# Gated linear attention with a gated projection behind it: scores and state sums of a chunk in 64-token halves, two batches at a time, in a new order of the work

## The chip, the cores and the metric

One of the eight cores of a Trainium2 chip runs the kernel. The metric is the device time of one execution in microseconds (us), taken as the median of several. The engines are PE (TensorE: matrix products, with PEld for the loading of their weights), DVE (VectorE), ACT (ScalarE), POOL (GpSimd) and SP (SyncE, which here only issues DMAs). Each works through its own instructions in order and waits on semaphores for the others.

## The reference

```python
B, H, S, D = q.shape                      # 4, 8, 768, 48
f = 1.0 / (1.0 + np.exp(-f_logit))
for t in range(S):                        # state: [B, H, D, D]
    state = f[:, :, t, :, None] * state + np.einsum('bhd,bhe->bhde', k[:, :, t], v[:, :, t])
    y[:, :, t] = np.einsum('bhd,bhde->bhe', q[:, :, t], state)
x = y.transpose(0, 2, 1, 3).reshape(B, S, H * D)          # 384 channels
gate = 1.0 / (1.0 + np.exp(-causal_conv(x, conv_w)))      # 5 taps, each channel alone
out = ((gate * (x @ w_val)) @ w_out).astype(np.float32)
```

The recurrence runs over 768 tokens for each of 32 (batch, head); the projection with its convolution takes its result. Everything is float32.

## The kernel before

**Chunks.** The 768 tokens are cut into 6 chunks of 128 (`C`). Heads go in pairs, one head on partitions 0 to 47 and the other on 64 to 111, so that there are 16 (batch, pair), `BP`, four pairs in each of four batches. q, k and f lie in HBM as 112 rows of 16 x 128 numbers to a chunk, v as 128 rows (tokens) of 16 x 112. In a chunk, ACT makes -log f (`pexp`, `pln`), DVE sums it along the tokens (`scan`), ACT makes the products of f (`exp1`, in `E1`) and one over them (`exp2`, in `E2`), and DVE multiplies q and k with them (`pmulq`, `pmulk`). These work on halves of 8 (batch, pair), three smaller spans in the first chunk.

**Batches.** What follows goes batch by batch, 24 times in all (chunk c, batch b):

- `scores`: eight products of 48 rows, k times q, 128 tokens against 128 tokens, into the two banks `aps`; `mask`: DVE multiplies all 128 x 1024 of them with the triangle `tri` into `ASB`.
- `ktrans`: four transposes of k into the bank `kps`; `kevac`: ACT copies them out to `KSB`. `dstate`: k times v summed over the 128 tokens into the bank `dps`, two batches side by side.
- For two batches together, `stadd` (DVE) adds `dps` to the state `ss`, `stmul` (POOL) multiplies with the chunk's decay, and `stcopy` (ACT) copies the two heads as blocks of a diagonal into `st`.
- `apply`: y from the state (`st` times q) and from the chunk's own tokens (v times `ASB`), in four lanes of 32 output rows, into one of two banks `xps`; `xevac`: ACT copies y into `XF`.

**The projection.** For each chunk, in three blocks of 128 channels: the convolution (`mlast` on ACT, then four `mconv` on DVE into `gt`), its sigmoid (`gate`), the value product `mval` (nine products of 128 x 128 by 128 x 512: x and w_val are each split in a high and a low part, `xH`, `xL`, `wvH`, `wvL`, by `msplit` and `mlow`), `mmul` on DVE, the split of the result (`mhigh` on ACT, `mrest` on DVE), the output product `mout` (nine products) and `mstore` (ACT, then a DMA). The last chunk's projection is done in two halves of two batches, which the program numbers 5 and 6, in 256 columns. The weights come as float64 bits and are turned into two float32 parts by POOL, ACT and DVE (`weight`). All these products write to two banks `mps`, in the last chunk also to the banks that the others have left.

**Order.** The list `PROGRAM` names the pieces one by one. PE, DVE and ACT do their pieces in exactly this order (class `Ordered`; hence nearly all instructions of the profile carry that helper's line, L113, and are told apart by their tiles' names). SP and POOL get their instructions from the framework's scheduler. All loads and stores go through SP, with at most eight DMAs under way: each waits for the eighth before it to land.

At the end a count tells whether every decay stayed in range; if not, a slow general path computes all anew. It isn't taken here.

Of the kernel before, what the change touches and what calls it, by code (L numbers as in the profile page):

```python
# [21 lines left out]
C = 128  # L22
NC = S // C
BP = B * NP
KT = 5
HALO = KT - 1
NM = DM // 128
#: a chunk's decay products have to stay above this for q * e and k / e to be formed apart
RANGE = 2.0**-58
# [3 lines left out]
WHOLE = [(0, BP)]  # L33
# [3 lines left out]
PROGRAM = """  # L37
halo 0; loadf 0 0; loadf 0 1; busy 10; loadq 0 1; loadq 0 0; loadk 0 0; loadv 0 0; pexp 0 0; loadk 0 1; loadq 0 2;
pln 0 0; loadf 1 0; scan 0 0; loadv 0 1; pexp 0 1; busy 4; loadk 0 2; exp2 0 0; pln 0 1; wload 0; exp1 0 0; busy 4;
loadk 1 0; pmulk 0 0; pexp 0 2; loadq 1 0; pmulq 0 0; ktrans 0 0; loadv 0 2; scan 0 1; pln 0 2; scores 0 0; exp2 0 1;  # L40
scan 0 2; wload 1; exp1 0 1; busy 4; kevac 0 0; pmulq 0 1; exp2 0 2; dstate 0 0; pmulk 0 1; busy 4; exp1 0 2;
mask 0 0; loadv 1 0; ktrans 0 1; loadf 2 0; okc 0; kevac 0 1; pmulq 0 2; scores 0 1; pexp 1 0; weight 0; pmulk 0 2;
apply 0 0; pln 1 0; mask 0 1; loadf 3 0; loadk 2 0; dstate 0 1; wload 2; ktrans 0 2; scores 0 2; kevac 0 2; scan 1 0;
xevac 0 0; stadd 0 0; exp2 1 0; ktrans 0 3; mask 0 2; apply 0 1; kevac 0 3; pmulk 1 0; scores 0 3; stcopy 0 0;
scan 1 1; xevac 0 1; exp1 1 0; ktrans 1 0; loadk 2 1; mask 0 3; apply 0 2; exp2 1 1; loadq 2 0; pmulq 1 0; exp1 1 1;
apply 0 3; loadv 2 0; weight 1; weight 0; xevac 0 2; weight 0; pmulq 1 1; scores 1 0; xevac 0 3; weight 1; halo 1;
msplit 0; weight 1; loadq 2 1; weight 1; dstate 0 2; mask 1 0; dstate 0 3; kevac 1 0; ktrans 1 1; weight 0; stadd 0 1;
scores 1 1; kevac 1 1; pmulk 1 1; loadv 2 1; pexp 2 0; weight 0; weight 1; dstate 1 1; weight 1; apply 1 0; okc 1;
mask 1 1; weight 1; loadf 4 0; pln 2 0; weight 1; mlow 0; weight 3; ktrans 1 2; loadk 3 0; scores 1 2; xevac 1 0;
stcopy 0 1; scan 2 0; apply 1 1; mask 1 2; exp2 2 0; exp1 2 0; weight 0; scan 2 1; weight 2; scores 1 3; loadq 3 0;  # L50
mlast 0 0; pmulk 2 0; xevac 1 1; weight 2; exp2 2 1; mconv 0 0 0; dstate 1 0; mask 1 3; apply 1 2; loadv 3 0;
kevac 1 2; exp1 2 1; pmulq 2 0; ktrans 1 3; pmulq 2 1; scores 2 0; loadk 3 1; kevac 1 3; xevac 1 2; mconv 0 0 1;
weight 3; mlast 0 1; stadd 1 0; ktrans 2 0; weight 2; mlast 0 2; dstate 1 2; stmul 1 0; weight 3; dstate 1 3;
# [12 lines left out]
exp1 4 0; weight 6; mask 3 2; mhigh 0 1; mhigh 0 0; mrest 0 1; dstate 3 1; loadq 5 0; weight 6; mrest 0 0; scores 3 3;
mhigh 0 2; loadv 5 0; weight 6; mlast 1 0; mrest 0 2; mlast 1 1; pmulk 4 0; mout 0 1; msplit 1; mconv 1 0 0;
mconv 1 0 1; mlast 1 2; mout 0 0; mconv 1 1 0; mstore 0 1; mconv 1 0 2; mconv 1 1 1; mout 0 2; mstore 0 0; mlow 1;
ktrans 3 2; mconv 1 0 3; mval 1 0; kevac 3 2; mconv 1 1 2; mstore 0 2; mconv 1 2 0; gate 1 0; stadd 3 0; ktrans 3 3;
mconv 1 1 3; stmul 3 0; mval 1 2; loadk 5 1; mconv 1 2 1; gate 1 1; mmul 1 0; stcopy 3 0; mconv 1 2 2; mval 1 1;  # L70
mhigh 1 0; mconv 1 2 3; kevac 3 3; stcopy 2 1; scan 4 1; halo 3; xevac 3 0; dstate 3 3; xevac 3 1; pmulq 4 0;
dstate 3 2; gate 1 2; apply 3 2; exp2 4 1; stadd 3 1; okc 3; mask 3 3; stmul 3 1; ktrans 4 0; mmul 1 2; pexp 5 0;
scores 4 0; mrest 1 0; mmul 1 1; pmulk 4 1; apply 3 3; mhigh 1 1; mhigh 1 2; mask 4 0; kevac 4 0; exp1 4 1;
dstate 4 0; mrest 1 1; loadq 5 1; mlast 2 0; scores 4 1; loadv 5 1; mrest 1 2; stcopy 3 1; mconv 2 0 0; pln 5 0;
mconv 2 0 1; mout 1 1; mask 4 1; msplit 2; scan 5 1; ktrans 4 1; mout 1 2; xevac 3 2; pmulq 4 1; exp2 5 1; mlow 2;
exp1 5 1; scores 4 2; kevac 4 1; mstore 1 1; pmulq 5 1; mlast 2 2; ktrans 4 2; mout 1 0; kevac 4 2; mconv 2 2 0;
mlast 2 1; mconv 2 0 2; xevac 3 3; scan 5 0; apply 4 0; mconv 2 0 3; exp2 5 0; mconv 2 1 0; exp1 5 0; dstate 4 1;
mconv 2 1 1; apply 4 1; gate 2 0; mask 4 2; pmulk 5 1; mstore 1 0; scores 4 3; mconv 2 2 1; mconv 2 2 2; mval 2 0;
mask 4 3; mstore 1 2; mconv 2 1 2; mval 2 1; mconv 2 2 3; mmul 2 0; pmulq 5 0; mhigh 2 0; ktrans 4 3; mval 2 2;
pmulk 5 0; kevac 4 3; gate 2 2; okc 4; stadd 4 0; scores 5 0; stmul 4 0; msplit 3; mmul 2 2; mconv 2 1 3; mrest 2 0;  # L80
mhigh 2 2; halo 4; dstate 4 2; xevac 4 0; dstate 4 3; mrest 2 2; stcopy 4 0; apply 4 2; stadd 4 1; xevac 4 1;
stmul 4 1; gate 2 1; mlast 3 2; mmul 2 1; apply 4 3; xevac 4 2; mask 5 0; mlast 3 0; mconv 3 0 0; apply 5 0;
mconv 3 0 1; xevac 4 3; mhigh 2 1; mconv 3 0 2; stcopy 4 1; mlow 3; scores 5 1; okc 5; mrest 2 1; mval 3 1; mlast 3 1;
mask 5 1; mconv 3 0 3; mval 3 0; mconv 3 2 0; gate 3 0; mconv 3 2 1; mconv 3 2 2; scores 5 2; mmul 3 0; mconv 3 2 3;
mval 3 2; mask 5 2; mconv 3 1 0; scores 5 3; msplit 4; mconv 3 1 1; mconv 3 1 2; gate 3 2; apply 5 1; mconv 3 1 3;
mmul 3 2; gate 3 1; halo 5; mmul 3 1; mout 2 0; xevac 5 1; mask 5 3; xevac 5 0; mlast 5 2; mlow 4; msplit 5; mout 2 2;
mlast 5 1; mstore 2 0; mlast 5 0; mconv 5 1 0; mlow 5; mout 2 1; mconv 5 0 0; mconv 5 0 1; mconv 5 2 0; mconv 5 0 2;
apply 5 3; mconv 5 1 1; mhigh 3 1; mconv 5 2 1; mhigh 3 2; mhigh 3 0; mrest 3 2; mconv 5 0 3; apply 5 2; mlast 4 2;
mrest 3 1; mstore 2 1; mconv 5 2 2; xevac 5 3; mrest 3 0; mconv 5 1 2; mlast 4 0; mval 4 0; mconv 5 1 3; mconv 4 0 0;
gate 5 1; xevac 5 2; mconv 4 0 1; mstore 2 2; mval 5 0; mlast 6 1; mconv 4 0 2; mlast 6 2; msplit 6; mout 3 0;  # L90
mconv 6 2 0; mconv 4 0 3; mlast 6 0; mlast 4 1; mconv 6 0 0; gate 4 0; mconv 6 0 1; mval 5 2; mconv 4 1 0; mstore 3 0;
# [33 lines left out]
def gla_moe(ctx: ExitStack, tc: tile.TileContext, q, k, f, v, wv, cw, wo, out):  # L125
# [292 lines left out]
    def general(ctx):  # L418
# [21 lines left out]
        for t in (qf, kf, ff):  # L440
            DVE.memset(t, 0.0)
# [203 lines left out]
```

## Time and profile before

| | us |
|---|---|
| time, median of 3 (lowest, highest) | 220.92 (220.72, 226.4) |
| span of the profiled execution | 227.6 |
| PE busy | 184.2 |
| DVE busy | 191.7 |
| ACT busy | 144.0 |
| POOL busy | 32.4 |

For the profiled execution the page gives its span, from the first to the last instruction, and no other time; that span lies 3.0% above the median of the timed runs and 0.5% above the highest. "Busy" counts the time in which at least one instruction of the engine was under way. PE's products overlap one another in their pipeline, so that its busy time is more than the sum of the steps from one product to the next. A float32 product shows as two records of PE, a transpose as one.

### The profile page before, as it was taken

The numbers are of one execution on the slowest core, as the hardware profiler recorded it, in microseconds if no ns is written. First come the engines' busy times: TensorE is split into PE (matmuls) and PEld (weight loads), VectorE is DVE, ScalarE is ACT, GpSimd is POOL, SyncE is SP. The second block draws the span as 40 slices with busy tenths as digits, with TensorE's granted clock in tenths as the row PEclk, the third lists the DMA queues.
The fourth block names the chain that finished last, engine by engine and source line by source line (L and its number), as shares of the span: only waits on it lengthen the run. The fifth ranks groups of instructions, "written<-read, shape, count | busy, mean of one in ns | idle before, by whom it ended". The sixth has DMA issues, their size and how long they took to land.

```text
span 227.6 us, 5654 instructions
## 1 busy us (share of the span) xinstructions
PE 184.2 (81%) x2437; PEld 148.5 (65%) x2438; DVE 191.7 (84%) x251; ACT 144.0 (63%) x226; POOL 32.4 (14%) x37
## 2 busy tenths in 40 slices
PE   7298689649198847775999987979879999999990
PEld 3156568438087736665787875767867788889880
DVE  5395989497499999999997999997799999998800
ACT  4677764686249298967639998553941858553630
POOL 4001011200044842240115100001200000000000
PEclk9959959976979999998599999979999999999998
DMA  6999999999959902244023050120000012111241
GB/s 190 280 254 268 333 336 278 238 239 258 240 129 278 250 15 84 81 164 143 21 92 128 3 164 0 49 95 0 4 3 0 1 49 79 62 50 42 103 152 37
DMA packets 9183, 29.54 MB, mean 130 GB/s; under 512 B 1200, under 2 KB 2224, under 8 KB 8112
## 3 DMA queue, kind: packets, MB, share of 16 engines
q1 hardware_dynamic: 9152, 29.12, 44.5%
q8 instruction: 21, 0.34, 0.6%
q14 instruction: 10, 0.08, 0.1%
HBM read 24.39 MB, written 4.72 MB: 128 GB/s over the span
## 4 chain that ended last, share of the span: by engine, by line
DVE 33%; PE 27%; DMA 24%; ACT 9%; issue 3%; SPq 2%; DVEq 0%; ACTq 0%
PE mps L113 19%; DMA qb<-in_q 10%; DVE gt L113 10%; DMA vb<-in_v 9%; DVE e L113 6%; DMA fb<-in_f 5%; DVE asb L113 5%; ACT e L113 3%; PE aps L113 3%; DVE qb L113 2%; DVE cb L113 2%; PE xps L113 2%; DVE ca L113 2%; DVE kb L113 2%; SPq L178 2%
## 5 line engine op out<-in xcount | busy, mean ns | idle before, releaser
L113 ACT ACTIVATE e<-e 112x1024 f32<-112x1024 f32 (+3 forms) x40 | 39.9, 1003 | 15.0 <-DVE e L113 14.6
L113 DVE SCALAR_TENSOR_TENSOR gt<-xf,cws,gt 128x512 f32<-128x512 f32 x60 | 45.2, 772 | 0.6
L113 PE MATMUL aps<-qb,kb 48*128 48x128 f32 x384 | 31.5, 310 | 13.3 <-DVE asb L113 11.9
L113 PE MATMUL xps<-asb,vb 128*32 128x128 f32 x768 | 38.2, 293 | 1.1 <-DMA vb<-in_v 0.7
L113 PEld LDWEIGHTS aps<-qb,kb 48*128 48x128 f32 x384 | 26.6, 210 | 19.0 <-DVE asb L113 14.2
L113 PE MATMUL xps<-qb,st 112*32 112x128 f32 x480 | 31.7, 287 | 4.7 <-issue 2.9
L113 PEld LDWEIGHTS xps<-asb,vb 128*32 128x32 f32 x768 | 32.8, 119 | 2.6 <-DMA vb<-in_v 1.0
L113 DVE TENSOR_TENSOR_SCAN e<-keep,e 112x1024 f32<-112x1024 bf16 (+1 forms) x13 | 28.7, 2218 | 5.2 <-ACT e L113 5.0
L113 PE MATMUL mps<-rg,woH 128*128 128x512 f32 (+1 forms) x102 | 32.3, 401 | 0.3 <-DVE gt L113 0.3
L113 DVE TENSOR_TENSOR asb<-aps,tri 128x1024 f32<-128x1024 f32 x24 | 29.1, 1213 | 0.0
L113 PEld LDWEIGHTS xps<-qb,st 112*32 112x32 f32 x480 | 22.2, 114 | 7.4 <-issue 3.9
L113 PEld LDWEIGHTS mps<-rg,woH 128*128 128x128 f32 x102 | 19.1, 199 | 4.6 <-DVE gt L113 0.5
L113 PE MATMUL mps<-xH,wvH 128*128 128x512 f32 x45 | 19.2, 428 | 3.1 <-DVE gt L113 2.9
L113 PE MATMUL mps<-rg,woL 128*128 128x512 f32 (+1 forms) x51 | 20.1, 395 | 0.0
L113 DVE TENSOR_TENSOR kb<-kb,e 112x1024 f32<-112x1024 f32 (+1 forms) x13 | 15.4, 1184 | 5.2 <-DMA kb<-in_k 5.2
L113 PE MATMUL mps<-xL,wvH 128*128 128x512 f32 x45 | 18.5, 410 | 0.9 <-DVE xL L113 0.9
L351 POOL TENSOR_TENSOR ss<-u,e 112x384 f32<-112x384 f32 x8 | 9.4, 1173 | 67.2 <-DVE u L113 63.3
L113 DVE TENSOR_TENSOR qb<-qb,e 112x1024 f32<-112x1024 f32 (+1 forms) x13 | 14.7, 1130 | 4.6 <-DMA qb<-in_q 4.6
L113 PE MATMUL mps<-xH,wvL 128*128 128x512 f32 x45 | 18.5, 411 | 0.0
L113 PE MATMUL dps<-vb,ksb 128*48 128x48 f32 x320 | 11.7, 226 | 7.6 <-DVE u L113 5.1
L113 PEld LDWEIGHTS dps<-vb,ksb 128*48 128x48 f32 x320 | 9.7, 137 | 11.5 <-DVE u L113 5.3
L113 ACT ACTIVATE e<-fb 112x2048 f32<-112x2048 f32 (+2 forms) x8 | 11.8, 1481 | 8.3 <-DMA fb<-in_f 8.2
(107 smaller groups left out, 301.8 us busy)
## 6 DMA issues: line engine op xcount, KB each, us to landing
fb<-in_f SPq DMA_DIRECT2D x5, 896.0 KB, 19.1
qb<-in_q SPq DMA_DIRECT2D x9, 448.0 KB, 8.1
kb<-in_k SPq DMA_DIRECT2D x9, 448.0 KB, 11.6
vb<-in_v SPq DMA_DIRECT2D x9, 448.0 KB, 9.4
out<-osb SPq DMA_DIRECT2D x15, 256.0 KB, 2.0
raww<-in_wv SPq DMA_DIRECT2D x1, 1152.0 KB, 19.8
raww<-in_wo SPq DMA_DIRECT2D x1, 1152.0 KB, 26.7
kb<-in_k SPq DMA_DIRECT2D x1, 896.0 KB, 13.5
```

Source lines behind the costliest of these rows:

```text
L113: ins = emit(*a, **kw)
L178: nc.sync.dma_start(dst[c % NB][: src.shape[1], x0:x1], src[c, :, x0:x1])
L351: nc.gpsimd.tensor_tensor(out=ss[:, HS[h]], in0=U[h][:], in1=decay(c, h), op=ALU.mult)
```

## The change

**What it does.**

- *64-token halves.* `scores` multiplies only tokens of one half (u = 0 or 1) with tokens of the same half: per (batch, pair) four products of 64 x 64, head s and half u each in its own quarter of PE's rows and columns, the two heads stacked on the 128 partitions. The second half's tokens see the first half's through a state in the middle of the chunk: `dstate` sums k times v over each half of 64 tokens (u = 0 the first, u = 1 the second; none for the second half of the last chunk), `stmid` adds the first to the state, `MID`, and `stend` the second; `stmul` is the decay as before.
- *One packed state.* The state is kept once, as 64 columns to a (batch, pair) (32 that both heads share, 32 of each head's own), in two buffers `ST`; `ss`, `U`, `st` and `stcopy` are gone. v is laid out to match, with 160 columns in place of 112.
- *Two batches at a time.* All these pieces work on a half h of a chunk: two batches, 8 (batch, pair). `mask`, `kevac`, `xevac` and the state's pieces are called 12 times (chunk, half); the last chunk has no `stend` and no `stmul`. Their sums go to three `pairs` of banks, which `ktrans`, `dstate`, `scores` and `apply` take in turn (`pair`) and give back when they are copied out (`done`).
- *128-row loads.* q, k and f have 128 rows in HBM and in the loads (112 are used). f is loaded into `E1` itself; the buffers `fb` are gone.
- *New order.* `PROGRAM` is another list. The stores' DMAs (`out`) and the final count (`check`) are pieces of it.

The pieces of the projection and their sizes are as before; `FOUR` is empty, so the code under it isn't built.

```diff
-    aps = ps.tile([C, 2, NP, C], F32, name="aps")
-    xps = [ps.tile([128, NM + 1, C], F32, name=f"xps{i}") for i in range(2)]
-    kps = ps.tile([C, NP, C], F32, name="kps")
-    dpb = ps.tile([128, B * C], F32, name="dps")
+    pairs = [ps.tile([128, 2, 512], F32, name=f"pair{i}") for i in range(3)]
...
+    for t in pairs:
+        DVE.memset(t[32:64], 0.0)
...
+    def pair(*key):
+
+        held[key] = spare.pop(0)
...
+    def ktrans(c, h):
+
+
+        t = pair("k", c, h)
+        for i in range(HP + 1):
             for s in range(2):
...
+                at = h * KH + (i * C if s == 0 else i % HP * C + HC)
+                PE.transpose(t[:, s, i * D : i * D + D], kb[c % NB][rows(s), at : at + C], ident[rows(s), rows(s)])
+
+    def kevac(c, h):
+        ACT.copy(KSB[slot(c, h)][:].rearrange("t s a d -> t s (a d)"), held["k", c, h][:, :, 0 : (HP + 1) * D])
+        done("k", c, h)
+
+    def dstate(c, h):
+
+        t, ks = pair("d", c, h), KSB[slot(c, h)]
+        for i in range(HP):
+            vt = vb[c % NB][:, h * HP + i]
+            for u in range(2 if c < NC - 1 else 1):
+                for s in range(2):
+                    r = slice(HC, C) if s == u else slice(0, HC)
...
+                    PE.matmul(t[rows(s), u, i * HC : i * HC + HC], ks[r, s, i + (u if s == 0 else 0)], vr, start=True,
+                              stop=True, tile_position=(r.start, s * HC))
+
+    def stmid(c, h):
+
+        t = held["d", c, h][:112, 0].rearrange("p (a e) -> p a e", e=HC)
+        DVE.tensor_tensor(out=MID[:, HS[h]], in0=ST[c % 2][:, HS[h]], in1=t, op=ALU.add)
...
+    def stend(c, h):
+        t = held["d", c, h][:112, 1].rearrange("p (a e) -> p a e", e=HC)
+        DVE.tensor_tensor(out=ST[(c + 1) % 2][:, HS[h]], in0=MID[:, HS[h]], in1=t, op=ALU.add)
...
+    def scores(c, h):
+        t, qt = pair("s", c, h), qb[c % NB]
+        kt = kview(c, h * HP, (h + 1) * HP)
+        for i in range(HP):
+            for u in range(2):
+                w = slice(u * HC, u * HC + HC)
+                for s in range(2):
+                    at = HC if s == u else 0
+                    PE.matmul(t[at : at + HC, u, i * HC : i * HC + HC], kt[rows(s), i, w],
+                              qt[rows(s), h * HP + i, w], start=True, stop=True, tile_position=(s * 64, at))
+
+    def mask(c, h):
+        DVE.tensor_tensor(out=ASB[slot(c, h)][:], in0=held["s", c, h][:].rearrange("p u (a t) -> p u a t", t=HC),
+                          in1=tri[:].unsqueeze(1).unsqueeze(1).to_broadcast([C, 2, HP, HC]), op=ALU.mult)
+        done("s", c, h)
...
-        y = np.full((NC, 112, BP, C), pad, x.dtype)
+        y = np.full((NC, 128, BP, C), pad, x.dtype)
```

`apply` first does 48 products of 32 x 64 (64 rows, the own columns of each head: from `ST` for the first half's tokens, from `MID` and from v for the second's) in eight lanes, two of rows by four of columns, then 48 over all rows in four lanes. In the first chunk, where the state is zero, there are 32 and 40.

**Where instructions stand now.** At the start SP loads what the first chunks need; `fb` or `e` is f, `raww` the projection's weights, and the number behind a name is the buffer. SP before, from its first row:

```order
L178 DMA fb_68<-in_f 112x512
L178 DMA fb_68<-in_f 112x1536
L178 DMA qb_64<-in_q 112x512 x2
L178 DMA kb_66<-in_k 112x512
L178 DMA vb_70<-in_v 128x448
L178 DMA kb_66<-in_k 112x512
L178 DMA qb_64<-in_q 112x1024
L178 DMA fb_69<-in_f 112x2048
```

SP now, from its first row:

```order
L645 DMA e_81<-in_f 128x512
L645 DMA e_81<-in_f 128x1536
L220 DMA rawcw<-in_cw 128x54
L645 DMA e_82<-in_f 128x2048
L220 DMA raww_93<-in_wv 128x2304
L645 DMA kb_66<-in_k 128x1024
L645 DMA kb_66<-in_k 128x512
L645 DMA qb_64<-in_q 128x1024
```

The f of the first two chunks and the first projection weight now stand ahead of every q, k and v, which before came between the first chunk's f and the second's.

On PE, in the first chunk, the pieces for two batches (before) and for one half of two batches (now). `aps` and the like are the banks named above; `x8` counts products, of which float32 ones make two records each. PE before:

```order
L113 MATMUL kps<-ident,kb_66 128x112 x4
L113 MATMUL aps<-qb_64,kb_66 128x128 x8
L113 MATMUL xps_105<-asb_84,vb_70 32x128 x16
L113 MATMUL dps<-vb_70,ksb_87 48x48 x8
L113 MATMUL kps<-ident,kb_66 128x112 x4
L113 MATMUL aps<-qb_64,kb_66 128x128 x8
```

PE now:

```order
L114 MATMUL pair_99<-ident,kb_66 128x48 x18
L114 MATMUL pair_100<-qb_64,kb_66 64x64 x32
L114 MATMUL pair_101<-ident,kb_66 128x48 x18
L114 MATMUL pair_99<-vb_68,ksb_87 48x64 x32
L114 MATMUL pair_101<-vb_68,ksb_86 48x64 x32
L114 MATMUL pair_100<-qb_64,mid 32x64 x8
L114 MATMUL pair_100<-asb_85,vb_68 32x64 x8
```

The products are smaller and more, the state's sums come ahead of `apply`, which now needs `mid`, and every piece takes one of the same three pairs of banks.

On DVE, in the third chunk, from the product of the second half of k with its decay (`kb`) to the additions to the state (`u<-ss,dps` before, for the first two batches; `mid` and `st` now, `pair_101` for the first half and `pair_99` for the second). `gt` with `cws` is `mconv`, `xL` is `mlow`, `ca` and `cb` belong to `weight`. DVE before:

```order
L113 TENSOR_TENSOR kb_66<-kb_66,e_83 112x1024
L113 SCALAR_TENSOR_TENSOR gt<-xf_90,cws,gt 128x512
L113 SCALAR_TENSOR_TENSOR ca_100<-raww_95,cb_101 128x384
L113 SCALAR_TENSOR_TENSOR cb_103<-ca_102,cb_103 128x384
L113 TENSOR_TENSOR asb_85<-aps,tri 128x1024
L113 SCALAR_TENSOR_TENSOR gt<-xf_90,cws,gt 128x512 x3
L113 TENSOR_TENSOR u_88<-ss,dps 112x384
```

DVE now:

```order
L114 TENSOR_TENSOR kb_66<-kb_66,e_83 112x1024
L114 TENSOR_TENSOR qb_64<-qb_64,e_81 112x1024
L114 TENSOR_SCALAR okc<-e_81 112x16
L114 TENSOR_TENSOR mid<-st_73,pair_101 112x512
L114 TENSOR_TENSOR xL<-xf_89,xH 128x1536
L114 SCALAR_TENSOR_TENSOR gt<-xf_89,cws,gt 128x512
L114 TENSOR_TENSOR qb_64<-qb_64,e_81 112x1024
L114 TENSOR_TENSOR st_74<-mid,pair_101 112x512
L114 SCALAR_TENSOR_TENSOR gt<-xf_89,cws,gt 128x512
L114 TENSOR_TENSOR mid<-st_73,pair_99 112x512
```

Before, one addition took the sums of two batches; now there are two additions to each half, `mid` and `st`. Between the product with k and the addition of its own sums (`mid` from `pair_99`) DVE now has eight other instructions.

More of the change, by code (lines that the diff above doesn't have):

```diff
@@ L33 @@
 WHOLE = [(0, BP)]
+FOUR = ()
 PROGRAM = """
[L38 to L41, printed above, removed]
@@ new lines @@
+1 0; mrest 1 0; mhigh 1 1; mrest 1 1; mhigh 1 2; mrest 1 2; mout 1 1; stmid 3 1; mlast 2 0; stend 3 0; mlast 2 2;
+mconv 2 2 0; scores 3 0; mconv 2 0 0; stend 3 1; mlast 2 1; mconv 2 1 0; loadv 4 1; loadq 4 1; loadv 4 0; mask 3 1;
+mask 3 0; pmulk 4 1; msplit 2; mlow 2; mconv 2 1 1; mout 1 0; mstore 1 1; exp1 4 1; out 1 1; exp2 4 0; exp1 4 0;
+mstore 1 0; mout 1 2; mstore 1 2; halo 3; apply 3 1; xevac 3 1; mval 2 2; ktrans 4 1; mval 2 1; stmul 3 0; stmul 3 1;
+loadf 5 0; pexp 5 0; pln 5 0; out 1 2; out 1 0; apply 3 0; mconv 2 0 1; mconv 2 2 1; mconv 2 1 2; pmulq 4 0; mconv 2 2
@@ L289, in mask @@
-    def mask(c, b):
-        DVE.tensor_tensor(out=ASB[slot(c, b)][:], in0=aps[:],
-                                in1=tri[:].unsqueeze(1).unsqueeze(1).to_broadcast([C, 2, NP, C]), op=ALU.mult)
-    def ktrans(c, b):
-        for p in range(NP):
-            PE.transpose(kps[:, p, 0:112], kb[c % NB][:, b * NP + p], ident[:112, :112])
-    def kevac(c, b):
-        ACT.copy(KSB[slot(c, b)][:].rearrange("t p h d -> t (p h) d"),
-                       kps[:].rearrange("t p (h d) -> t (p h) d", h=2)[:, :, 0:D])
@@ new lines, in gla_moe, with done @@
+    HS = [slice(h * HP, (h + 1) * HP) for h in range(2)]
+    slot = lambda c, h: (2 * c + h) % 2
+    rows = lambda s: slice(s * 64, s * 64 + D)
+    held, spare, free, uses = {}, list(pairs), list(mps), [8 * NC]
+    def pair(*key):
+        held[key] = spare.pop(0)
+        uses[0] -= 1
+        return held[key]
+    def done(*key):
+        spare.append(held.pop(key))
+        while len(spare) > uses[0]:
+            t = spare.pop(0)
+            free.extend([t[:, 0], t[:, 1]])
+    def ktrans(c, h):
+        t = pair("k", c, h)
+        for i in range(HP + 1):
+            for s in range(2):
+                at = h * KH + (i * C if s == 0 else i % HP * C + HC)
+                PE.transpose(t[:, s, i * D : i * D + D], kb[c % NB][rows(s), at : at + C], ident[rows(s), rows(s)])
@@ L378, in mconv, with xload, mfour, mfifth @@
                                            op1=ALU.add)
+    def xload(n, j):
+        src = XF[n % 2]
+        size = B * TH - j
+        for g in range(4):
+            nc.sync.dma_start(X4[j * 32 : j * 32 + 32, :, g].rearrange("p m b t -> p m (b t)")[:, :, 0:size],
+                              src[g * 32 : g * 32 + 32].rearrange("p m b t -> p m (b t)")[:, :, j:])
+    def mfour(w, m, bank):
+        w["pc", m] = bank
+        for g in range(4):
+            PE.matmul(bank[g * 32 : g * 32 + 32, : w["n"]], W4[:, m, g], X4[:, m, g, w["b"], 0:C], start=True, stop=True,
+                      tile_position=(0, g * 32))
+    def mfifth(w, m):
+        DVE.scalar_tensor_tensor(out=w["gt"][:, m], in0=w["xf"][:, m, w["b"], HALO:],
+                                 scalar=cws[:, m * KT + HALO : m * KT + KT],
+                                 in1=w["pc", m][:, : w["n"]].rearrange("p (b t) -> p b t", t=C), op0=ALU.mult, op1=ALU.add)
     def mgate(w, m):
@@ L502, in gla_moe @@
     N2 = NM * 2 * C
-    proj, late, held, free, stored = {}, {}, {}, list(mps), []
-    ap2 = [flat(aps[:, n]) for n in range(2)]
-    banks = {("mval", last): [*ap2, flat(kps)], ("mout", last): [None, None, ap2[0]],
-             ("mval", NC): [dpb, *[flat(x) for x in xps]], ("mout", NC): [ap2[1], flat(kps), dpb]}
+    proj, late, stored, bufs = {}, {}, [], {}
     def retag(tag, n):
```

432 lines of the change are left out of this document (239 added, 193 removed).

## Prediction

> **What bounds the kernel now.** I first cut the span into stages, to see which engine has no room in which. The columns are busy time and instructions of PE, PEld, DVE, ACT and POOL, PE's granted clock, the DMA engines' busy share and GB/s.
>
> ```profile
> core 0: us, PE busy (x) PEld busy (x) DVE busy (x) ACT busy (x) POOL busy (x), PEclk, DMA share, GB/s
> 0.00:20.00 20.00, 14.37 (x105) 8.02 (x110) 12.19 (x17) 12.35 (x19) 2.51 (x11) 0.83 0.92 245
> 20.00:40.00 20.00, 16.50 (x316) 13.44 (x304) 18.22 (x22) 13.12 (x20) 2.57 (x4) 0.83 1.02 309
> 40.00:60.00 20.00, 12.19 (x196) 9.84 (x188) 12.36 (x10) 13.78 (x20) 1.54 (x2) 0.83 1.02 243
> 60.00:200.00 140.00, 119.65 (x1707) 98.28 (x1708) 134.52 (x171) 94.16 (x144) 25.83 (x20) 0.95 0.27 82
> 200.00:227.60 27.60, 21.47 (x135) 18.94 (x133) 14.44 (x34) 10.63 (x25) 0.00 (x0) 0.97 0.22 79
> ```
>
> Up to 60 us the DMA engines are full and DVE stands still for 7.8 + 1.8 + 7.6 us. From 60 to 200 DVE is the bound: 134.5 of 140 us busy. At the end it stands still for 13.2 us. Next the chain that ended last, in order of time, for the end (start, us, what):
>
> ```profile
> 175.21 1.13 DVE asb L113
> ...
> 180.02 6.57 PE mps L113 x27
> 186.59 3.21 PE xps L113 x112
> ...
> 210.85 7.32 PE mps L113 x36
> 218.17 1.06 PE dps L113 x9
> ...
> 221.38 0.37 ACT fb L113
> ```
>
> From the last mask on (`asb`) PE works off a backlog of projection blocks without a gap; after the last copy, at 221.75, another 5.8 us pass. So there are three bounds in turn: loads, DVE, and PE in the last 41 us.
>
> **DVE's work.** These groups carry it (count | busy us, mean ns | idle before):
>
> ```profile
> L113 DVE TENSOR_TENSOR asb<-aps,tri 128x1024 f32<-128x1024 f32 x24 | 29.1, 1213 | 0.0
> L113 DVE TENSOR_TENSOR u<-ss,dps 112x384 f32<-112x384 f32 x8 | 4.4, 546 | 0.0
> L113 DVE TENSOR_TENSOR ss<-dps,e 112x384 f32<-112x384 f32 x2 | 1.1, 539 | 0.0
> L113 DVE TENSOR_TENSOR gt<-mps,gt 128x512 f32<-128x512 f32 x15 | 10.2, 685 | 4.5 <-ACT gt L113 2.6 <-PE mps L113 1.8
> L113 DVE MEMSET dps<- 32x384 f32 x1 | 0.4, 378 | 0.1
> L113 DVE MEMSET keep<- 112x1524 bf16 x1 | 1.3, 1328 | 0.2 <-DVE keep L113 0.2
> ```
>
> - Masks: 12 of the same size in place of 24, -12 x 1.213 = -14.6 us.
> - State: 12 `stmid` and 10 `stend` of 112 x 512, one operand in PSUM. The trace has none of that size; the nearest rows are `u` (384 columns, 0.546) and `gt<-mps` (512, 0.685). I take 0.69, the row of equal width: +15.2, less the 5.5 of `u` and `ss`: +9.7. With 0.546 it would be +6.5.
> - Memsets: three of 32 x 1024 at 0.378 x 1024/384 = 1.0 each; the one of `dps` goes, and `keep` shrinks by 0.9 (1.328 and a first part of 0.485 against 0.9): +1.7, all before the first f has landed.
>
> The scans, products with q and k, and the whole projection are the same instructions. Sum: 191.7 - 14.6 + 9.7 + 1.7 = **188.5 us** busy. Of DVE's work alone the change takes 3.2 us; the rest has to come from its idle 35.9 us.
>
> **Loads.** There is more to load: q, k and f grow by 128/112, v by 160/112, together from 22.0 to 26.7 MB, and with the weights from 24.4 to 29.1. What a byte costs depends on the load's shape. The first two lines are the DMAs between 18 and 24 us, the others between 26 and 30:
>
> ```profile
> DMA packets 235, 1.62 MB, mean 270 GB/s; under 512 B 33, under 2 KB 33, under 8 KB 43
> q1 hardware_dynamic: 234, 1.60, 100.2%
> ...
> DMA packets 216, 1.60 MB, mean 400 GB/s; under 512 B 19, under 2 KB 19, under 8 KB 110
> q1 hardware_dynamic: 216, 1.60, 99.1%
> ```
>
> In both the queue is full. In the first, 192 of the 202 larger packets have 8 KB or more: rows of 2048 numbers, that is k, q and f with 112 rows. In the second there are v (rows of 7 KB) and the raw weights (9 KB), both of 128 rows. So 112 rows go at 270 GB/s and 128 rows at 400. At 400, all of the first two chunks and both weights (11.3 MB) are in after some 30 us; the `q` that DVE waits for at 60 us is that of the third chunk:
>
> ```profile
> DVE qb L113 <- DMA qb<-in_q: 4.6, 1, 4.6
> DVE kb L113 <- DMA kb<-in_k: 5.2, 2, 3.6
> DVE e L113 <- ACT e L113: 5.5, 4, 3.2
> ACT e L113 <- DMA fb<-in_f: 8.2, 3, 4.1
> ```
>
> With 4.5 MB to a chunk at 400 GB/s it would come by about 42 us if its buffers are free. I count the waits for loads after 20 us as gone. What is late next is the first chunk's chain, below.
>
> **PE.** Steps in full flow (start, us, engine, tiles, records), and the transposes from the chain:
>
> ```profile
> 176.91 1.16 PE L113 MATMUL aps<-qb,kb 48*128 48x128 f32 x16
> 178.00 0.43 PE L113 MATMUL xps<-qb,st 112*32 112x128 f32 x8
> 160.02 0.93 PE L113 MATMUL dps<-vb,ksb 128*48 128x48 f32 x32
> 156.49 0.38 PE kps L113 x4
> ```
>
> Scores of one batch take 1.09 us to the next piece, `apply` 1.6 (3.21 for two), a record of `dps` 29 ns (two side by side in 58), a transpose 95 ns, a projection block 2.19 (6.57 / 3), a half block 1.06. Before: 24 x 1.09 + (20 x 1.6 + 4 x 0.9) + 320 x 0.029 + 80 x 0.095 = 78.7, and 30 x 2.19 + 12 x 1.06 = 78.4 for the projection: 157. Now the attention has 768 records of scores, 704 of state sums, 2208 of `apply` and 216 transposes. No 64-column product is in the trace; from below its step is the 58 ns of 48 columns, from above the 136 ns of a pair of scores of 128 (1.09 / 8). I take 58, the nearer width, with four at a time for scores and sums, eight or four for `apply` (136 + 280 steps), two for transposes: 11.1 + 10.2 + 24.1 + 10.3 = 56, with the projection **134 us**. That stays below DVE's 188.5, so what PE saves isn't saved time in the middle; it only empties the backlog at the end.
>
> **DVE's idle time after.**
>
> Rows for this part:
>
> ```profile
> L113 DVE SCALAR_TENSOR_TENSOR gt<-xf,cws,gt 128x512 f32<-128x512 f32 x60 | 45.2, 772 | 0.6
> L113 DVE SCALAR_TENSOR_TENSOR e<-xf,cws,e 128x256 f32<-128x256 f32 x24 | 11.0, 480 | 0.2
> L113 DVE TENSOR_TENSOR qb<-qb,e 112x1024 f32<-112x1024 f32 x11 | 13.3, 1213 | 4.6 <-DMA qb<-in_q 4.6
> L113 DVE TENSOR_TENSOR xL<-xf,xH 128x1536 fp32r<-128x1536 f32 x5 | 8.7, 1749 | 0.0
> L113 ACT ACTIVATE e<-fb x8: 629/1904/1914, 3.7 to 128.2; 112x2048 f32<-112x2048 f32 x5, 112x512 f32<-112x512 f32 x2, 112x1024 f32<-112x1024 f32 x1
> L113 ACT COPY osb<-mps 128x512 f32<-128x512 f32 x15 | 8.5, 583 | 8.5 <-PE mps L113 6.2 <-issue 2.3
> L113 ACT ACTIVATE e<-e 112x1024 f32<-112x1024 f32 x23 | 24.3, 1057 | 13.3 <-DVE e L113 13.0
> L113 ACT COPY st<-ss 48x384 f32<-48x384 f32 x20 | 10.2, 509 | 6.7 <-POOL ss L351 6.5
> ```
>
> - 0 to 20 us: 7.8 less the 1.7 of memsets that now lie in the wait for f: 6.1. The f comes as early as before and passes through the same ACT pieces.
> - 20 to 60: 9.4 go. New is the first chunk's chain, where little else is ready: transposes 0.9, their copy by ACT 0.9 (864 columns, between 512 at 0.58 and 1024 at 1.06, as `osb` and `e` take above), state sums 0.9, scores 0.9, before the additions and the masks. PE's clock was 0.83 there and PE now rests longer: between 3.6 at full and 6.3 us at half clock, for two halves; the weights' pieces cover a part. I take 6, bounds 2 and 12.
> - 60 to 200: 5.5 as before, bounds 3 and 12. The cover for a half's chain: behind the second half's product with k, eight DVE instructions stand before its `mid` (the change's rows): two `qb` at 1.2, `xL` 1.7, two `gt` at 0.8, the other half's `mid` and `st` at 0.7, `okc`: 7.2 us, against 2.7 for transposes, copy and sums at full clock. Were one of these `mid` late, what stands behind it on DVE (`xL`, `gt`) would wait too, and PE's `apply` for it. f now goes into `E1` and so waits until POOL has used that buffer's decay; behind it on SP stand the next v and k. From there its chain is 2.6 + 2 us of load and twice 1.9 on ACT; the order gives it over 10 us of DVE's work each time.
> - The end: behind the last mask PE has nine whole and twelve half blocks and one `apply`: 9 x 2.19 + 12 x 1.06 + 2 = 34.4 us, where from the last mask's end at 176.3 to the last block's at 221.4 it took 45; DVE has 12 `gt` at 45.2 / 60 and 24 `e<-xf` at 11.0 / 24, 20 us, and some 13 of smaller pieces. So they end together; behind DVE's last subtraction come three half blocks, a copy and the 5.8: 3.2 + 0.4 + 5.8 = 9.4, and 0.6 of waits: 10.
>
> The 20 copies `st<-ss`, 10.2 us of ACT, are gone too; ACT, 144 us busy, isn't the bound, and I count them at nothing. DVE hides them; were its cover gone they'd be worth at most those 10.
>
> Sum: 6.1 + 6 + 5.5 + 10 = 27.6 idle, and 188.5 + 27.6 = 216.1 us for the profiled execution, against 227.6. That execution lies above the timed ones, so I carry over the ratio: 220.92 x 216.1 / 227.6 = **209.8 us**, -5.0%.
>
> **Rivals.**
>
> 1. *Two row groups on one bank take turns.* The scores' two heads, and the sums' two halves of tokens, come from different rows of PE and write the same bank. In the trace the scores' two heads wrote a bank each and ran side by side (16 records in 1.16 us), so no row shows it. Taking turns costs PE 11.1 + 10.2 = 21 us more, 155 in all, and each half's chain 1.8 us; the cover of 7 us hides most, the first chunk doesn't (3.7, at half clock 7.5). I price it at +6: 222, or 215.6 us. The page TensorEngine Tiling (Array Packing) of the Trainium skill, under Restrictions and Gotchas, says so: different row tiles cannot access one PSUM bank at the same time. By that rule the sum would be this rival's.
> 2. *DVE finds nearly all ready:* idle 18 (5 + 2 + 3 + 8), 206.5, or 200.5 us. For it: from 60 to 200 us DVE was idle for 3.9% only.
> 3. *128 rows bring nothing,* the 400 GB/s being due to what was under way just then. At 270, 19% more bytes put the third chunk's data some 10 us later than now; the 9.4 us of waits stay and grow: 226 to 229, or 219 to 222. Against it: both windows have a full queue.
> 4. *Slower: PE becomes the bound,* as small products cost as much as large ones. Now a record of the attention costs 78.7 / 2032 = 39 ns. With 3896 records and the projection's 78.4, 39 ns make 230 and with 12 at the ends 242, or 235 us. It decides from 36 ns on (3896 x 0.036 + 78.4 + 12 = 231, or 224); I forecast 14. Against it: `dps`, narrow and two abreast, already runs at 29 a record.
> 5. *The shared pairs make DVE wait:* each of the 48 uses of three pairs must be copied out by ACT or DVE before a third next; 1 us at a third of them gives 232, or 225. Before, PE waited for the masks' single buffer (10 times, up to 2.6 us), yet DVE waited for PE's products for only 1.8 us in all (the `gt<-mps` row).
>
> ```profile
> PEld aps L113 <- DVE asb L113: 14.2, 10, 2.6
> ```
>
> **Chances.** Forecast (204 to 214) 0.48; rival 1 0.15 (213 to 219); 2 0.14 (199 to 204); 3 0.07; 4 0.07; 5 0.09 (214 to 230). The range from 200 to 220 leaves out 4, most of 5, half of 3 and a bit of 2. Faster by over 2% (below 216.5; about what timing can tell from no change): 0.72; within 2%: 0.18; slower: 0.10.
>
> **What would show it.** In the profile after: DVE at 187 to 190 us busy and the first engine by share; `asb` 12 times at 1.2; `mid` and `st` at 0.69; no wait of DVE for a DMA after 25 us; over 350 GB/s while loads queue; 64-column scores under 20 ns a record (about 29 by rival 1); DVE ending less than 11 us before the span's end. Most likely to be wrong is the first chunk's 6 us and the waits in the middle, which I could only bound.

## The result, and the profile after

The changed kernel is **slower**: 227.94 us median of 4 runs (225.65 to 230.43) against 221.12, ratio 1.030 with a 95% interval of 1.022 to 1.039. The prediction said 209.8, range 200 to 220. (Ratios here are taken from undisturbed runs alone, so that they need not equal the quotient of two medians; the profile below is of the longest of the four executions.)

The stages first, with the columns of the prediction's first view (PE, PEld, DVE, ACT, POOL busy; PE's granted clock; DMA share; GB/s):

```profile
core 0: us, PE busy (x) PEld busy (x) DVE busy (x) ACT busy (x) POOL busy (x), PEclk, DMA share, GB/s
0.00:20.00 20.00, 4.33 (x10) 1.31 (x10) 15.84 (x21) 14.27 (x21) 5.78 (x22) 0.72 0.91 354
20.00:40.00 20.00, 13.42 (x532) 11.87 (x536) 15.21 (x24) 6.89 (x11) 6.11 (x6) 0.67 0.80 309
40.00:60.00 20.00, 12.76 (x417) 10.83 (x408) 17.67 (x24) 13.29 (x18) 4.22 (x5) 0.59 0.56 191
60.00:200.00 140.00, 115.94 (x3193) 93.77 (x3194) 117.44 (x139) 88.22 (x119) 27.10 (x14) 0.90 0.34 113
200.00:228.70 28.70, 22.22 (x149) 19.78 (x147) 18.96 (x48) 12.37 (x30) 0.00 (x0) 0.97 0.16 58
```

DVE stands still for 4.2 us up to 20, 7.1 up to 60, 22.6 from 60 to 200 and 9.7 at the end: 43.6 us. Forecast were 6.1, 6, 5.5 and 10. One stage is off, the one in which DVE was the bound before. What DVE waited for, over the whole span (us, times, longest):

```profile
DVE asb L114 <- PE pair L114: 11.0, 4, 4.1
DVE gt L114 <- ACT gt L114: 8.1, 5, 4.0
DVE gt L114 <- PE mps L114: 5.8, 1, 5.8
DVE re L114 <- ACT re L114: 2.1, 1, 2.1
```

Of the 22.6 us from 60 to 200, 13.9 ended on PE (8.1 in `asb`, 5.8 in `gt`) and 8.3 on ACT, which itself stands behind PE's results (its copies `xf` wait 28.5 us for `pair` over the span). The chain of work that ended last shows what stands there now; "issue" is time in which PE waited for nothing that the profile shows:

```profile
105.96 2.00 PE pair L114 x123
107.96 2.42 issue
110.38 0.87 PE pair L114 x44
111.25 3.84 PE mps L114 x9
...
126.16 2.35 PE pair L114 x148
128.50 5.19 issue
```

Twice PE stops in the middle of an `apply`, between two products of one series, and no wait for an operand shows. The waits of PE by what they end on (us, times, longest), first after, then before:

```profile
PE pair L114 <- issue: 20.4, 14, 5.2
```
```profile
PE xps L113 <- issue: 2.9, 1, 2.9
```

So 20.4 us of stops without a visible cause, where before's longest group had 2.9. What else grew is in the lists of DMA queues, after and before:

```profile
q8 instruction: 35, 0.57, 1.1%
```
```profile
q8 instruction: 21, 0.34, 0.6%
```

A packet of that queue has 16 KB. PE has 4286 product records and as many weight loads now, 8572, and had 4875: 245 and 232 to a packet. Counted along PE's records, products and weight loads together, the first stops lie at 443, 699, 954, 1209, 1463 and 1718, some 255 apart, and later ones at 5028, 5539, 6047, 6558, 7068 and 7577, some 510 apart: one and two blocks of 256, if a few records are missing from the trace. That gave the theory.

**Theory: instruction supply.** PE's instructions come in blocks of 256. A block is asked for when PE enters the one ahead of it, so a block must hold work for as long as the next takes to come. **Rivals:** *clock or array* (PE is late since its clock is low, 0.847 in this execution, or since its work is too much); *order* (PE waits for banks and for DVE).

### The profile page after: what moved, and what is told of

The parts are those of the page before. It is cut to its first block, busy times and chain, and to the rows that moved or that the text cites. A ratio compares the mean times of both kernels' runs of the same rounds, so it can differ in the third digit from the quotient of the medians.

```text
span 228.7 us, 9386 instructions
## 1 busy us (share of the span) xinstructions
PE 168.7 (74%) x4286; PEld 137.6 (60%) x4286; DVE 185.1 (81%) x252; ACT 135.0 (59%) x198; POOL 43.2 (19%) x47
## 4 chain that ended last, share of the span: by engine, by line
PE 45%; DVE 32%; issue 13%; ACT 5%; DMA 2%; SPq 0%; DVEq 0%
PE pair L114 26%; PE mps L114 19%; DVE e L114 11%; DVE gt L114 6%; DVE rg L114 3%; DVE kb L114 3%; DVE qb L114 2%; DMA e<-in_f 2%; DVE work L114 2%; DVE mid L114 2%; DVE xL L114 1%; ACT e L114 1%; DVE st L114 1%; ACT gt L114 1%; DVE re L114 1%
## 5 line engine op out<-in xcount | busy, mean ns | idle before, releaser
L114 PE MATMUL pair<-asb,vb 128*32 128x64 f32 (+1 forms) x1152 | 28.8, 237 | 7.1 <-issue 6.1
L362 POOL TENSOR_TENSOR st<-st,e 112x512 f32<-112x512 f32 x10 | 25.1, 2515 | 38.2 <-PE mps L114 24.5
L114 PEld LDWEIGHTS pair<-asb,vb 128*32 128x32 f32 (+1 forms) x1152 | 22.3, 118 | 9.8 <-issue 8.6
L114 ACT COPY xf<-pair 128x512 f32<-128x512 f32 (+1 forms) x24 | 10.2, 484 | 28.5 <-PE pair L114 28.5
L114 PE MATMUL mps<-rg,woH 128*128 128x512 f32 x78 | 25.4, 406 | 0.0
L114 DVE TENSOR_TENSOR asb<-pair,tri 128x1024 f32<-128x1024 f32 x12 | 14.5, 1216 | 11.0 <-PE pair L114 11.0
L114 PE MATMUL pair<-vb,ksb 64*48 64x64 f32 x704 | 16.2, 241 | 7.1 <-issue 4.9
L114 PE MATMUL pair<-qb,mid 48*32 48x64 f32 (+1 forms) x576 | 18.3, 239 | 3.1 <-issue 2.6
L114 PEld LDWEIGHTS pair<-vb,ksb 64*48 64x48 f32 x704 | 14.2, 139 | 9.6 <-issue 6.3
L114 PE MATMUL pair<-qb,kb 48*64 48x64 f32 x768 | 16.1, 236 | 4.8 <-issue 3.1
L114 ACT COPY ksb<-pair 128x864 f32<-128x864 f32 x12 | 10.4, 876 | 14.4 <-PE pair L114 14.4
L114 PE MATMUL pair<-qb,st 48*32 48x64 f32 (+1 forms) x480 | 14.9, 240 | 2.4 <-issue 2.4
```

The source lines that it names most:

```text
L114: ins = emit(*a, **kw)
L362: nc.gpsimd.tensor_tensor(out=s, in0=s, in1=E1[c % NB][:112, HS[h], C - 1 : C].to_broadcast([112, HP, HC]), op=ALU.mult)
```

## The experiments

**1. The supply by itself.** PE alone, with the scores' products (48 rows, 64 x 64, four quarters) in four stages; `small` is 32 products, `wide(9)` nine whole ones of 512 columns (the edit in outline):

```diff
+    for n in range(16): small(n)                    # stage 1: 16 x 32 products in a row
+    for n in range(16): small(n); wide(9) if n % 2  # stage 2
+    for n in range(16): small(n); wide(9)           # stage 3
+    (18 loads of 1 MB); for n in range(16): small(n)  # stage 4
```

> This kernel leaves the whole computation out and runs PE alone: pieces of 32 float32 products of 64 columns, as the scores of one half (128 instructions, 0.95 us in the changed kernel at full clock), on constant tiles without a wait. Stage 1: 16 pieces in a row. Stage 2: nine wide products (1.9 us) behind each second piece. Stage 3: nine wide ones behind each piece. Stage 4: 16 pieces in a row while 18 loads of 1 MB run. Theory 'instruction supply' (PE's instructions come in blocks of 256, and a block takes 3.4 to 4.0 us to come when the DMA engines are quiet, 5 to 8 when they are full): stage 1 takes 27 to 32 us, with a gap of 1.5 to 2 us in each 256 instructions; stage 2 about 31 us, with little or no gap, though it does twice the work; stage 3 about 46 us without gaps; stage 4 40 to 64 us. Rival 'array' (products cost what they cost in flow, and the gaps of the changed kernel have another cause): stage 1 15 to 16 us without gaps, stage 2 31, stage 4 the same as stage 1.

Three rows of PE's timeline from stage 1 and four from stage 4 (start, length, count of product records, idle time ahead of it):

```profile
20.91 2.09 PE L114 MATMUL pair<-qt,kt 48*64 48x64 f32 x128 [1.18 <-issue]
24.64 2.09 PE L114 MATMUL pair<-qt,kt 48*64 48x64 f32 x128 [1.64 <-issue]
28.09 2.09 PE L114 MATMUL pair<-qt,kt 48*64 48x64 f32 x128 [1.36 <-issue]
...
163.47 3.32 PE L114 MATMUL pair<-qt,kt 48*64 48x64 f32 x128 [3.50 <-issue]
169.67 3.69 PE L114 MATMUL pair<-qt,kt 48*64 48x64 f32 x128 [2.87 <-issue]
...
182.06 3.69 PE L114 MATMUL pair<-qt,kt 48*64 48x64 f32 x128 [2.51 <-issue]
188.26 3.69 PE L114 MATMUL pair<-qt,kt 48*64 48x64 f32 x128 [2.51 <-issue]
```

No wait is in this program, and PE stops after each 128 products and 128 weight loads. A block takes **3.45 us** to the next (28.09 - 24.64) with quiet DMA engines and **6.2 us** (188.26 - 182.06) with full ones (412 GB/s from 160 to 200 us). The time of the work in a block doesn't move that step: early in stage 4 a block with 3.32 us of work and the next stop of 2.87 make 6.2 too. Stage 1 took 26.6 us, just under the expected 27 to 32; stage 2, with the same products and 63 wide ones in between, 30.8, with no stop above 0.3 us; stage 3 48.4, as free of stops; stage 4 45.5. The rival's 15 to 16 us for stage 1 is out. What an instruction may cost without a stop follows: 3.45 / 256 = 13.5 ns, or 27 ns for a product record with its weight load, and 48 with the queues full. An `apply` spends 2.59 us on 384.

The stops stand at the same counts as in the changed kernel: behind records 446, 702 and 958 here, 443, 699 and 954 there. Ahead of the first of them PE had spent 16 us on wide products, and still little lay ready. So blocks aren't laid up far ahead, as the theory has it. No run separates its rule (one block ahead) from other ways to limit the supply.

The Trainium skill has this under Runtime: NRT & Kernel Launch, Instruction fetch mechanics: instructions are refilled in blocks of 16 KiB while the present one runs, and crossing into a block is mostly hidden. The blocks and their size agree with the trace. Hidden it isn't in stages 1 and 4, at 1.4 to 2.5 us a block; in stages 2 and 3 it is.

**2. Fewer instructions, as much work.** In each `apply` the second loop makes room for 13 wide products, so that y lacks its sums (in outline; the banks are also cleared whole at the start):

```diff
-        (48 products of 32 x 64 over all rows: 192 instructions)
+        for _ in range(13):
+            PE.matmul(t[:, 1, 256:512], idle[:, 0:128], idle[:, 0:256], start=True, stop=True)
```

> The changed kernel, but of each apply the second loop (48 products of 32 x 64 over all rows, 192 instructions, 1.45 us) is left out, and 13 products of 256 columns in bf16 into an unused part of the same bank (26 instructions, about 1.4 us) stand in its place. PE's array is as busy as before and everything else is the same, but PE has some 6600 instructions in place of 8600. Theory 'instruction supply': PE's idle time without a visible cause falls from 20.4 us to about 8 to 12, and the time to 216 to 222 us. Rivals 'clock or array' and 'order': 226 to 230 us.

Measured: **210.22 us**, ratio to before 0.954 (0.946 to 0.961). An `apply` took 2.64 us (129.02 to 131.66), so PE's work there takes as long as before (2.59), and the stops are

```profile
PE pair L114 <- issue: 4.0, 5, 1.5
```

16.4 us of stops went, and 17.7 us of time, more than expected (216 to 222). DVE is busy for 88% of this span, 184.0 of 209.3 us. Its row for the middle:

```profile
60.00:185.00 125.00, 112.86 (x2469) 90.81 (x2469) 119.12 (x144) 89.45 (x123) 25.70 (x14) 0.94 0.37 121
```

The order of the pieces is unchanged and PE's products take as long, so order and array are out as main causes. The granted clock is 0.874 for 0.847 over the span; experiment 5 takes it up.

**3. More instructions in the kernel before.** The same from the other side: ahead of each of before's 24 `apply` pieces some idle products, meant to take 0.85 us, once in 160 instructions, once in 32.

```diff
+        for n in range(80): PE.matmul(x_[z..z+32, NM, 0:64], idle[:, 0:32], idle[:, 0:64], ...)   # many
+        for n in range(16): PE.matmul(x_[:, NM], idle[:, 0:128], idle[:, 0:C], ...)               # few
```

> The kernel before, and ahead of each apply's products 80 small ones more (32 columns of weights, 64 moving, bf16, four lanes, into an unused part of the same bank): 160 instructions and about 0.85 us of PE's array each time, 3840 instructions in all, so that PE has some 8700, as many as in the changed kernel. Theory 'instruction supply': it stops as the changed kernel does, 15 to 25 us of idle time without a visible cause, and ends 8 us or more above the next kernel, at 232 to 245 us. Rival 'array': like the next kernel, 222 to 230 us.

> The kernel before, and ahead of each apply's products 16 products of 128 columns, bf16, over the whole array into the same unused part: again about 0.85 us of PE's array each time, but 768 instructions in all. Both theories: PE has 20 us more to do, of which the waits for DVE hide most: 222 to 230 us, with few stops without a visible cause.

Many: 249.74 us, ratio 1.117 (1.108 to 1.126). Few: 227.38, ratio 1.017 (1.008 to 1.026). Ten per cent lie between them, though many's idle products take less of PE's time at full clock than few's, 0.63 us a piece against 1.00. The stops of many (its profiled execution took 257.99 us), then of few:

```profile
PE xps L113 <- issue: 19.9, 11, 3.5
PE aps L113 <- issue: 8.0, 4, 3.8
```
```profile
PE xps L113 <- issue: 1.7, 2, 1.4
```

With 4.1 us in smaller groups, many's stops come to 32.0 us. Both they and its time lie above the forecast (15 to 25, and 232 to 245). They stand at the counts of the changed kernel, the first four at 444, 700, 955 and 1210. Not all of the 22 us between the two need be stops: from 20 to 60 us many's granted clock was 0.62, few's 0.93.

**4. Same instructions, dealt out.** The changed kernel, with eleven projection blocks mixed into pieces of the attention product by product; then eight whole blocks set between the two loops of an `apply` (in outline, one place of each):

```diff
-    mval 1 0; apply 2 0
+    apply 2 0 with a product of mval 1 0 behind each tenth of its own     # mixed
+    first loop of apply 2 0; mval 1 0; second loop of apply 2 0           # halved
```

> The changed kernel with the same instructions; only on PE, eleven products blocks of the projection that stood ahead of a piece of the attention are dealt out evenly between that piece's products (and one copy of a result stands a few pieces later on ACT). Theory 'instruction supply': a block of 256 instructions then holds more time of work, so PE's idle time without a visible cause falls from 20.4 us to 8 to 13, and the time from 227.9 to 218 to 223 us. Rival 'clock or array' (PE is late since its granted clock is 0.85 instead of 0.92, or since its work is too much): the work is the same, so 226 to 230. Rival 'order' (PE waits for banks and for DVE): the blocks of the projection end up to 2 us later, so 227 to 231.

Mixed: **260.92 us**, ratio 1.171 (1.155 to 1.186). All theories missed this, though the stops fell, to 4.4 us (8 to 13 expected). PE's timeline in a mixed `scores` shows why:

```profile
124.85 0.49 PE L120 MATMUL pair<-qb,kb 48*64 48x64 f32 x8 [2.64 <-DVE st L120]
125.27 0.79 PE L120 MATMUL mps<-rg,woH 128*128 128x512 f32 x1
125.99 0.49 PE L120 MATMUL pair<-qb,kb 48*64 48x64 f32 x8
126.42 0.79 PE L120 MATMUL mps<-rg,woH 128*128 128x512 f32 x1
```

A wide product takes 0.72 us to the next here, and 0.43 within a block at this halved clock; eight small ones take 0.42 for 0.24. Each change between tiled and whole products costs about a quarter of a microsecond at this clock. The Trainium skill says under TensorEngine Tiling (Array Packing), Key Properties, that a change of tiling mode drains the engine; the trace agrees in that each change costs time. Over the kernel PE's busy time rose by 38 us (168.7 to 206.9) for 99 products mixed in. The granted clock was 0.823 in place of 0.847, which can account for some 5 of them (an estimate: 168.7 x 0.847 / 0.823).

> The changed kernel with the same instructions; on PE alone, eight blocks of the projection stand in the middle of an apply, between its two loops, and not ahead of or behind it (one copy on ACT stands later). Theory 'instruction supply': some of the stops get 2.2 us of work inside the block that ran dry; PE's idle time without a visible cause falls from 20.4 to 11 to 15 us; each place costs one more change between tiled and whole products, about 0.4 us, 3 us in all; time 219 to 225 us. Rivals 'clock or array' and 'order': 227 to 231 us.

Halved: 222.37 us, ratio 1.007 (1.001 to 1.012), within the expected 219 to 225, and 2.3% less than the changed kernel's 1.030. The stops:

```profile
PE pair L119 <- issue: 9.3, 8, 1.7
PE mps L119 <- issue: 2.2, 2, 1.7
```

So the same instructions, in an order with more work in the blocks that ran dry, win back 5 us. It doesn't beat the kernel before.

**5. The clock.** Once the changed kernel again, for a profile of another execution; once the halved kernel with PE kept busy up to the first chunk.

```diff
-busy 10; loadf 0 0; ...
+busy 82; loadf 0 0; ...
```

> The changed kernel, unchanged, for a second profile, since the first one is of an execution with a granted clock of 0.847 and 2.5 us above the median. Theory 'instruction supply': the stops stand at the same places of the instruction stream, and PE's idle time without a visible cause is again 16 to 22 us. Rival 'clock': at a granted clock above 0.88 these stops shrink to under 10 us.

> The kernel with eight blocks of the projection inside the applies, and 82 wide products of zeros in place of 10 at the start, so that PE doesn't rest from 5 to 22 us. If the low granted clock in the first chunk (0.67 from 20 to 40 us) holds DVE up, its 4.6 us of waits for PE there halve: 219 to 221.5 us, against 222.4 without. If the stops for instructions set that stage, which take as long at either clock, the time stays at 221.5 to 224 us.

The second profile of the changed kernel (227.29 us, granted clock 0.855) has its stops at the same counts, 18.3 us in 13; its clock was too low to try the rival by the stops. The times on record do try it: two of the four executions of the changed kernel had a granted clock of 0.920 and 0.914 and still took 225.65 and 228.16 us. So does the warm start: 228.17 us, ratio 1.036 (1.017 to 1.056), where it should have gained or changed nothing. The stops of the one, then of the other:

```profile
PE pair L114 <- issue: 18.3, 13, 4.8
```
```profile
PE pair L119 <- issue: 20.2, 13, 3.4
```

From 20 to 60 us, the halved kernel's row, then that of the warm one:

```profile
20.00:60.00 40.00, 26.44 (x937) 23.08 (x938) 33.03 (x48) 20.41 (x30) 10.33 (x11) 0.63 0.70 257
```
```profile
20.00:60.00 40.00, 23.78 (x921) 19.91 (x921) 29.37 (x41) 18.29 (x26) 9.84 (x11) 0.75 0.62 234
```

A higher clock (0.75 for 0.63), and DVE does 3.7 us less: the stops there became longer, up to 3.4 us, and fell in other places, since 144 more instructions moved the blocks' edges by more than half a block. Over the whole span they came to 20.2 us at a granted clock of 0.913. So the low clock isn't the main cause. How much of the 6 us is the moved edges and how much the faster start stays open.

**6. The loads.** The load term alone in the kernel before, a second profile of that kernel, and the term undone in the changed kernel:

```diff
-        y = np.full((NC, 112, BP, C), pad, x.dtype)     # before
+        y = np.full((NC, 128, BP, C), pad, x.dtype)     # with tiles of 128 rows; the reverse in the changed kernel
```

> The kernel before, unchanged, for a second profile: the one that the prediction read has a span of 227.6 us, and 9 us above most runs of it. If the loads at 270 GB/s and DVE's 9 us of waits from 20 to 60 us were this execution's own, this profile shows loads at 350 to 420 GB/s, a span of 217 to 219 and idle time of DVE from 20 to 60 us of under 4 us; if they belong to the kernel, the same rates and waits stand here again.

> The kernel before, with one part of the change alone: q, k and f have 128 rows in HBM and in the loads (112 are used). The prediction's load term: while loads queue, 128 rows move at about 400 GB/s in place of 270, so DVE's waits for q, k, e of the third chunk (some 9 us of idle time from 20 to 60 us) go, and the time falls to 211 to 215 us. Rival 'the rows bring nothing': 14% more bytes at the same rate put the third chunk's data 4 to 6 us later: 224 to 228 us.

> The changed kernel with one part undone: q, k and f have 112 rows in HBM and in the loads again. By the load term of the prediction (270 against 400 GB/s) the loads of the first two chunks end some 8 us later; DVE's waits for loads in the first 60 us come back, 5 to 9 us, and the time is 232 to 237 us. As the same rows in the kernel before moved its time by 0.5% alone (1.3 us), the rival says 228 to 231 us.

The DMAs between 8 and 40 us, of the second profile of before, then with 128 rows:

```profile
DMA packets 2017, 9.64 MB, mean 301 GB/s; under 512 B 370, under 2 KB 587, under 8 KB 1281
```
```profile
DMA packets 2972, 13.48 MB, mean 421 GB/s; under 512 B 451, under 2 KB 707, under 8 KB 2074
```

The low rate is the kernel's own (few of experiment 3, which has the same loads, moved 298 GB/s in that window), and with 128 rows the DMAs move 421. From 40 to 60 us, in the same order:

```profile
40.00:60.00 20.00, 11.88 (x200) 9.80 (x198) 13.64 (x15) 11.73 (x18) 2.61 (x3) 0.79 1.03 241
```
```profile
40.00:60.00 20.00, 15.36 (x292) 13.03 (x291) 19.97 (x22) 13.36 (x22) 5.41 (x4) 0.83 0.50 188
```

DVE's 6.4 us of waits in that window are gone. Yet the time fell only to 219.33 us, ratio 0.995 (0.990 to 1.000); neither theory gave that. The two profiled executions differ by 3.3 us, 221.4 and 218.1, and before's was longer than most; why a wait of 6.4 us is worth so little stays open. Of the versions that compute the whole result it is the only one below the kernel before, by half a per cent, too little to be called faster. In the changed kernel the same edit undone costs far more, 239.38 us (236.35 to 240.58) beside a single 227.29 in the same comparison, and above both forecasts. The first 60 us, changed and then undone:

```profile
0.00:60.00 60.00, 30.51 (x947) 24.00 (x947) 48.73 (x67) 34.45 (x50) 16.12 (x33) 0.66 0.76 285
```
```profile
0.00:60.00 60.00, 23.98 (x720) 19.14 (x724) 37.60 (x52) 27.93 (x42) 15.39 (x31) 0.63 0.86 236
```

DVE does 11.1 us less there: PE's first transposes start 4 us later, at 26.3 for 22.2 (q and k stand behind f and the weights in the new order), and PE's longest stop in the first chunk takes 5.4 us, where with 128 rows none took over 1.7.

## Why the prediction was wrong

- **DVE's work:** 188.5 forecast, 185.1 measured. The masks took 1.216 us, `mid` and `st` 0.68. Right within 2%.
- **Loads, 0 to 60 us:** idle 11.3 for 12.1, and no wait of DVE for a DMA. Right as to the profile.
- **PE's array:** a `scores` piece and, behind it, a `dstate` piece in full flow:

```profile
115.94 1.11 PE L114 MATMUL pair<-qb,kb 48*64 48x64 f32 x64
116.88 1.07 PE L114 MATMUL pair<-vb,ksb 64*48 64x64 f32 x64
```

  `scores` takes 0.94 us to the next piece (64 records, 14.7 ns each; 14.5 forecast), `dstate` the same, a transpose 38 ns (48), `apply` 2.59 us (2.0): 60 us in place of 56. Rival 1 forecast 29 ns, so it falls. The rule of the Trainium skill that different row tiles cannot access one PSUM bank at once (TensorEngine Tiling (Array Packing), Restrictions and Gotchas) isn't borne out by this row: two of them write one bank here, at half the time a record that taking turns would give.
- **60 to 200 us: the step that failed.** "That stays below DVE's 188.5, so what PE saves isn't saved time in the middle" took PE's time for the time of its array, and the stage for "5.5 as before, bounds 3 and 12". It was 22.6. PE has 8572 instructions in place of 4875, and in attention pieces a block of 256 holds 1.7 to 1.9 us of work, half of what the supply takes. PE stood for 14.4 us in that stage, and DVE's masks and gates wait for its results. With most stops gone (experiment 2) DVE's idle time from 60 to 185 us, where that kernel's end begins, was 5.9 us, as forecast.
- **The end:** 9.7 us idle for 10.
- **The scaling was mis-sized too.** The profiled execution of before has a span of 227.6; runs of 219.4 to 221.6 us had spans of 216.6 to 218.9. So the 9.4 us of load waits that the sum takes away, and the factor 220.92 / 227.6, were from an execution some 9 us above the usual one. How long DVE waits for loads in a usual one no profile of that kernel shows. The load term alone was worth 1.3 us in the kernel before. Set against a usual span of 217.5, the same sum of 216.1 would have said "no change".
- **Rival 4** had the sign and the engine, at 0.07: PE becomes the bound as small products cost as much as large ones. Its price, 39 ns a record, was for all of them and came from the array. What the runs show is a floor of 27 ns (48 with full queues) on blocks that hold nothing else, and it came from the supply; the time lies between forecast and rival.
- Of the marks named: DVE as the first engine by share, GB/s, `asb`, `mid` and `st`, the missing DMA waits and the scores under 20 ns came; DVE ended 12 us before the end, not 11, and at 185.1 busy, below 187 to 190. None of the marks looked at PE's unexplained idle time, which the page of before shows at 2.9 us.

## What to carry to other kernels

Count an engine's instructions, not only its busy time: where a change cuts products into smaller ones, set every 256 of PE's instructions against the time that a block takes to come (3.45 to 6.2 us here), and look for "issue" waits that repeat at equal counts. Spread small pieces by whole blocks of large ones, not product by product. And take the sum against a profile that is as long as the runs it is to forecast.

## What was not expected of the hardware

- Blocks of 256 instructions in packets of 16 KB; 3.45 us from block to block with quiet DMA engines, 6.2 us beside loads at 412 GB/s, with blocks of small products. In the changed kernel, in many and in halved the first three stops stand at the same counts of PE's records (443 or 444, 699 or 700, 954 or 955).
- Between 0.3 and 0.4 us for a wide product set between tiled ones (38 us for 99 of them, some 5 of which the lower clock can explain).
- In experiment 1, PE kept its full granted clock (1.00) with stops of 1.4 us in 3.45. With full queues it fell from 1.00 to 0.50 behind a first stop of 3.50 us and stayed at 0.50 to 0.55 with stops of 2.5 us in 6.2.
